# Decode attention plus a gated feed-forward layer on one core: one tile for the gate's activation, and slots for loads that start 32 bytes earlier

## The chip, the core and the metric

The kernel runs on one core of a Trainium2 chip. The core has TensorE (matmuls; PE in the profile, PEld for its loads of weights), VectorE (DVE), ScalarE (ACT), GpSimd (POOL) and SyncE (SP), which here only issues loads. Sixteen DMA engines carry the data between the device's memory and the core's own memory. The core's memory has 128 partitions; a tile has a place in it that is the same byte offset in every partition.

The metric is the device time of one execution in microseconds (us), lower being better.

## The reference, cut to what matters

One token of width 576 is normalised. Attention has 32 heads of width 128 with 16384 cached keys and values each; the feed-forward layer has 4608 hidden units with a tanh-approximated GELU on its gate. All in float32. The output is the sum of the token, the attention and the feed-forward layer.

```python
q = (x @ wq).reshape(B, Sq, H, Dh).transpose(0, 2, 1, 3)          # H, Dh = 32, 128
scores = jnp.einsum("bhqd,bhkd->bhqk", q, k_cache) * (Dh ** -0.5)  # k_cache: 1 x 32 x 16384 x 128
p = _softmax(scores, axis=-1)
o = jnp.einsum("bhqk,bhkd->bhqd", p, v_cache)
A = o.transpose(0, 2, 1, 3).reshape(B, Sq, H * Dh) @ wo

h = _gelu(x @ w_gate) * (x @ w_up)                                  # 576 -> 4608
B = h @ w_down                                                      # 4608 -> 576

xn = _layernorm(x)
return x + A(xn) + B(xn)
```

The K and V caches are 32 x 16384 x 128 x 4 bytes each, 537 MB together, and are read once.

## The kernel before, in words

**Slots.** All large loads go into three slots of 65536 bytes per partition: two of the pool kpool (`kslot()`) and one of the pool vpool (`vslot()`). A load of one head's K or V fills a slot: partition p gets 128 consecutive rows of the cache, 65536 contiguous bytes. The pool cpool lies in front of the slots in each partition and holds the constants and small results; the pool spool (qs, s, the small softmax tiles, o4) lies behind them. A tile takes its bytes rounded up to a multiple of 32. With the tiles of cpool as they are, the first slot starts at byte 27680, the second at 93216 and the third at 158752; each is 32 bytes past a multiple of 1024.

**Loads.** `load()` (L69) issues every large load on SP's queue, in the order of the program. SP waits before a load until its slot is free. Ahead of the heads come the query weights, and the gate and up weights (8 loads; the third slot, `mix`, holds parts of gate and up). Each head has a load of K and one of V (K of head 0 in two halves, so 65 in all). After the heads come the down weights in pieces of 28 and 8 rows and the attention's output weights in pieces of 16, 8, 4, 2, 1 and 1 rows (8 loads), a row being 576 floats of each partition. Inside a slot every one of these loads begins at an offset that is a multiple of 256 bytes.

**One head.** For head h the loop at the end of the main part issues K of h and V of h - 1. Then VectorE multiplies K by the query in place (L215) and sums over the 128 elements of each key (L216); that is `qk`. `softmax` takes the maximum over partitions by way of TensorE (L220 to L226) and lets ScalarE write the exponentials into the tile `pe` (L228, L229), with their sums in a column of `lsum`. `pv` does 32 products of `pe` and V on TensorE (L236) for the head before. V's slot is free when these are done; a slot of K is free when VectorE has summed it. Every four heads `out_heads` collects the result.

**The activation.** `ffn_act` runs once, behind head 0's `qk` on VectorE. Its VectorE steps keep the program's order. It has the gate and up results in `gu` (36 columns of 128 partitions) and makes hT: three steps on VectorE into t1 (L189 to L191), a Tanh on ScalarE from t1 into th (L193), then VectorE's (th + 1) x gate into t2 (L195) and 0.5 x t2 x up into hT (L196).

**The end.** The sums of `lsum` are added over partitions (L300), the heads' results are scaled, and TensorE multiplies by the down and output weights (L281) as their pieces arrive.

Of the kernel before, what the change touches and what calls it, by code (L numbers as in the profile page):

```python
# [8 lines left out]
F32 = mybir.dt.float32  # L9
AF = mybir.ActivationFunctionType  # L10
ALU = mybir.AluOpType
AX = mybir.AxisListType

P = 128
H, SK, DH = 32, 16384, 128
# [11 lines left out]
WD_T = DF // P  # L27
# [7 lines left out]
QUART = D // 4  # L35
HG = 4
PW = 4 * HG
QH = 4


@with_exitstack
def kernel(ctx: ExitStack, tc: tile.TileContext, x, k_cache, v_cache, wq, wo, wg, wu, wd, out):
    nc = tc.nc
    cpool = ctx.enter_context(tc.tile_pool(name="cpool", bufs=1))
# [17 lines left out]
    def kslot():  # L62
        return kpool.tile([P, R * DH], F32, tag="k", name="kslot")

    def vslot():
        return vpool.tile([P, R * DH], F32, tag="v", name="vslot")

    def load(dst, src):
        nc.sync.dma_start(dst, src)  # L69
        return dst  # L70
# [79 lines left out]
    def q_spread(h):  # L150
        r = 32 * (h // (H // 4))
        lo = h % (H // 4) * DH
        pq = ps_s.tile([P, 512], F32, tag="sm", name="pq")
        nc.tensor.matmul(pq, ones[r : r + 1, :], qrow[r : r + 1, lo : lo + QH * DH], start=True, stop=True)  # L154
        return pq

    def q_take(h, pq):
        qs = spool.tile([P, QH, DH], F32, name="qs", bufs=1)
        nc.scalar.activation(qs.rearrange("p h d -> p (h d)"), pq, AF.Copy)
        for i in range(QH):  # L160
            Q[h + i] = qs[:, i : i + 1, :]
# [22 lines left out]
    hT = cpool.tile([P, WD_T], F32, name="hT")  # L184

    def ffn_act():
        g, u = gu[:, 0], gu[:, 1]
        t1 = cpool.tile([P, WD_T], F32, name="t1")
        tc.keep_in_program_order(nc.vector.tensor_mul(t1, g, g))  # L189
        tc.keep_in_program_order(nc.vector.tensor_scalar(t1, t1, 0.044715, 1.0, op0=ALU.mult, op1=ALU.add))  # L190
        tc.keep_in_program_order(nc.vector.tensor_mul(t1, t1, g))  # L191
        th = cpool.tile([P, WD_T], F32, name="th")
        nc.scalar.activation(th, t1, AF.Tanh, scale=0.7978845608028654)  # L193
        t2 = cpool.tile([P, WD_T], F32, name="t2")
        tc.keep_in_program_order(nc.vector.scalar_tensor_tensor(t2, th, 1.0, g, op0=ALU.add, op1=ALU.mult))  # L195
        tc.keep_in_program_order(nc.vector.scalar_tensor_tensor(hT, t2, 0.5, u, op0=ALU.mult, op1=ALU.mult))  # L196

    PO = [ps_o.tile([P, 512], F32, name=f"po{i}") for i in range(2)]
    acc = ps_acc.tile([P, 512], F32, name="acc")
# [3 lines left out]
    S, KT, VT = {}, {}, {}  # L203
    pe = cpool.tile([P, PW - 4 + 32 * PW], F32, name="pe")
    nc.vector.memset(pe, 0.0)
    pe4 = pe[:, PW - 4 :].rearrange("p (k s) -> p k s", s=PW)[:, :, :4]
    lsum = cpool.tile([P, H], F32, name="lsum")
    oall = cpool.tile([P, H], F32, name="oall")

    def qk(h, i, n):  # L210
# [21 lines left out]
    def pv(h):  # L232
        vt, i = VT.pop(h), h % HG
        for k in range(32):
            q, lo = 32 * (k % 4), k * PW + PW - 4 - 4 * i
            nc.tensor.matmul(PO[h // HG % 2][q : q + PW, :], pe[:, lo : lo + PW], vt[:, k * 512 : (k + 1) * 512],  # L236
                             start=i == 0 and k < 4, stop=i == HG - 1 and k >= 28)

    def out_heads(h):
        o4 = spool.tile([P, 512], F32, name="o4", bufs=1)  # L240
        nc.scalar.activation(o4, PO[h // HG % 2], AF.Copy)  # L241
        pc = ps_s.tile([P, 512], F32, tag="sm", name="pc")
        pick = same[:, :PW].rearrange("p (i j) -> p j i", j=4)
        for j in range(4):
# [4 lines left out]
    for h in range(H + 1):  # L249
        if h < H:  # L250
            KT[h], n = kslot(), R if h else SUB
            for i in range(0, R, n):
                load(KT[h][:, i * DH : (i + n) * DH], kv[h][:, i * DH : (i + n) * DH])
        if h > 0:
            VT[h - 1] = load(vslot() if h < H else kslot(), vv[h - 1])
        more = (h + 1) % QH == 0 and h + 1 < H
        pq = q_spread(h + 1) if more else None
        if h < H:
            for i in range(0, R, n):
                qk(h, i, n)  # L260
            KT.pop(h)
        if h == 0:
            ffn_act()
        if h > 0:
            pv(h - 1)
            if h % HG == 0:
                out_heads(h - HG)
        if more:
            q_take(h + 1, pq)
        if h < H:  # L270
            softmax(h)
# [86 lines left out]
```

## Time and profile before

| | us |
|---|---|
| time, median of 3 runs (1369.99 to 1370.04) | 1370.03 |
| the profiled execution's own time | 1370.16 |
| its span, first to last instruction | 1368.3 |
| VectorE busy | 1135.8 (83%) |
| TensorE busy with matmuls | 406.0 (30%) |
| ScalarE busy | 36.5 (3%) |
| moved by DMA | 588.00 MB, 430 GB/s over the span |

The page cuts the span into 40 equal slices; a digit is the busy share of a slice in tenths. A group line names the line of the kernel, the engine, the operation and its tiles; after the first bar come its total busy time and the mean in ns, after the second the idle time of the engine just ahead of it and what ended that. In a line of the chain the first number is the start and the second the duration, both in us. In the timeline, the square bracket gives the idle time before an instruction and what it had waited for. In a line of the windows come the stretch, its length, the busy time of PE, PEld, DVE, ACT and POOL with the number of instructions, the granted clock of TensorE, the share of the DMA engines and their GB/s. In a line of the waits stand the total in us, the number of waits and the longest.

### The profile page before, as it was taken

What the parts mean: (1) busy time and instruction counts of PE and PEld (TensorE: products, weight loads), DVE (VectorE), ACT (ScalarE), POOL (GpSimd) and SP (SyncE); (2) the same over time, 40 slices, a digit from 0 to 9 for tenths busy, and PEclk for the clock granted to TensorE, in tenths of its full rate; (3) what the DMA queues carried; (4) which work ended last, traced back from release to release, by engine and by line L of the source; (5) the groups of instructions that cost most, each with busy time, mean ns of one, the idle gap of its engine ahead of it and who ended that gap; (6) DMA issues with size and microseconds to landing.
All of it is one profiled execution on the core that took longest, in us unless ns stands there. A gap on an engine that the chain in (4) does not pass through costs nothing.

```text
span 1368.3 us, 6377 instructions
## 1 busy us (share of the span) xinstructions
PE 406.0 (30%) x2870; PEld 118.1 (9%) x2870; DVE 1135.8 (83%) x169; ACT 36.5 (3%) x126; POOL 1.0 (0%) x7
## 2 busy tenths in 40 slices
PE   4321233322311232323212332322213333221156
PEld 1110000100000000100000000100001000000012
DVE  1069999899888888898888888998888888988840
ACT  0000000000000000000000000000000000000000
POOL 0000000000000000000000000000000000000000
PEclk8775565565556556565566566565556555665577
DMA  9999999999999999999999999999999999999997
GB/s 404 440 425 450 430 429 430 430 435 432 437 435 429 431 430 439 432 432 435 431 436 433 433 431 430 435 432 439 435 430 430 431 432 437 438 435 428 429 428 336
DMA packets 11704, 588.00 MB, mean 430 GB/s; under 512 B 1303, under 2 KB 1309, under 8 KB 1694
## 3 DMA queue, kind: packets, MB, share of 16 engines
q1 hardware_dynamic: 11664, 587.60, 99.4%
q8 instruction: 22, 0.36, 0.1%
q14 instruction: 4, 0.03, 0.0%
q10 hardware_dynamic: 14, 0.01, 0.0%
HBM read 587.60 MB, written 0.00 MB: 429 GB/s over the span
## 4 chain that ended last, share of the span: by engine, by line
DMA 51%; DVE 46%; PE 2%; issue 0%; SPq 0%; ACT 0%; DVEq 0%
DMA kslot<-in_A_k_cache_dram 41%; DVE s L216 23%; DVE kslot L215 23%; DMA kslot<-in_A_v_cache_dram 3%; DMA kslot<-in_B_w_up_dram 3%; DMA kslot<-in_A_wo_dram 3%; DMA kslot<-in_A_wq_dram 2%; PE pg L139 1%; PE po L236 1%; DVE gu L179 0%; SPq L69 0%; PE pt L222 0%; DVE vslot L176 0%; DVE pm L220 0%; DVE nm L224 0%
## 5 line engine op out<-in xcount | busy, mean ns | idle before, releaser
L215 DVE TENSOR_TENSOR kslot<-kslot,qs 128x16384 f32<-128x16384 f32 (+1 forms) x33 | 551.3, 16705 | 88.4 <-DMA kslot<-in_A_k_cache_dram 86.9
L216 DVE TENSOR_REDUCE s<-kslot 128x128 f32<-128x16384 f32 (+1 forms) x33 | 551.2, 16703 | 3.3
L236 PE MATMUL po<-vslot,pe 128*16 128x512 f32 x1984 | 286.1, 741 | 645.0 <-DMA vslot<-in_A_v_cache_dram 645.0
L236 PEld LDWEIGHTS po<-vslot,pe 128*16 128x16 f32 x1984 | 67.3, 113 | 848.2 <-issue 848.2
L222 PE MATMUL pt<-ident,pm 128*1 128x128 f32 x32 | 11.9, 372 | 236.0 <-DVE pm L220 236.0
L176 DVE TENSOR_TENSOR vslot<-pg,same 128x396 f32<-128x396 f32 (+1 forms) x6 | 3.0, 552 | 69.1 <-PE pg L139 69.1
L139 PE MATMUL pg<-kslot,xnb 128*32 128x396 f32 (+2 forms) x208 | 23.6, 615 | 33.6 <-DMA kslot<-in_B_w_gate_dram 18.9
L228 ACT ACTIVATE nb<-pb 128x1 f32<-128x1 f32 x32 | 5.5, 171 | 812.4 <-PE pb L226 812.4
L320 DVE TENSOR_TENSOR x<-x,po 64x288 f32<-64x288 f32 x1 | 0.5, 457 | 30.8 <-PE po L281 30.8
L222 PEld LDWEIGHTS pt<-ident,pm 128*1 128x1 f32 x32 | 2.5, 79 | 259.4 <-DVE pm L220 218.5
L226 PE MATMUL pb<-nm,ones 1*128 1x1 f32 x64 | 18.1, 350 | 13.2 <-DVE nm L224 13.2
L224 DVE TENSOR_REDUCE nm<-pt 1x1 f32<-1x128 f32 x32 | 8.9, 278 | 14.9 <-PE pt L222 14.9
L226 PEld LDWEIGHTS pb<-nm,ones 1*128 1x128 f32 x64 | 15.8, 305 | 22.2 <-DVE nm L224 11.3
L154 PE MATMUL pq<-qrow,ones 1*128 1x512 f32 x16 | 15.6, 1073 | 0.0
L229 ACT ACTIVATE pe<-s,nb 128x128 f32<-128x128 f32 x32 | 12.8, 401 | 1.0
L302 DVE RECIPROCAL rl<-pl 128x32 f32<-128x32 f32 x1 | 0.4, 358 | 14.9 <-PE pl L300 14.9
L281 PE MATMUL acc<-kslot,oT 128*1 128x144 f32 (+1 forms) x112 | 10.5, 376 | 6.7 <-DMA kslot<-in_A_wo_dram 6.7
L139 PEld LDWEIGHTS pg<-kslot,xnb 128*32 128x32 f32 x208 | 7.1, 126 | 51.0 <-DMA kslot<-in_B_w_gate_dram 19.7
L241 ACT ACTIVATE o<-po 128x512 f32<-128x512 f32 x8 | 4.8, 597 | 222.0 <-PE po L236 222.0
L236 PE MATMUL po<-kslot,pe 128*16 128x512 f32 x64 | 9.6, 769 | 2.6 <-DMA kslot<-in_A_v_cache_dram 2.6
L281 PE MATMUL acc<-vslot,hT 128*1 128x288 f32 x56 | 8.6, 473 | 5.6 <-DMA vslot<-in_B_w_down_dram 5.6
L245 PE MATMUL pc<-same,o 128*128 128x4 f32 x64 | 8.4, 255 | 5.7 <-ACT o L241 5.7
(74 smaller groups left out, 109.9 us busy)
## 6 DMA issues: line engine op xcount, KB each, us to landing
kslot<-in_A_k_cache_dram SPq DMA_DIRECT2D x2, 4096.0 KB
vslot<-in_B_w_down_dram SPq DMA_DIRECT2D x1, 8064.0 KB
kslot<-in_B_w_gate_dram SPq DMA_DIRECT2D x1, 6912.0 KB, 54.0
kslot<-in_B_w_up_dram SPq DMA_DIRECT2D x1, 6912.0 KB
kslot<-in_A_wo_dram SPq DMA_DIRECT2D x1, 4608.0 KB, 39.2
vslot<-in_B_w_gate_dram SPq DMA_DIRECT2D x1, 2304.0 KB, 28.9
vslot<-in_B_w_up_dram SPq DMA_DIRECT2D x1, 2304.0 KB, 37.6
kslot<-in_B_w_down_dram SPq DMA_DIRECT2D x1, 2304.0 KB, 28.7
```

What stands on the lines that cost most here:

```text
L139: nc.tensor.matmul(pg[32 * q : 32 * q + 32, b, :size], lhs, rhs[:, lo : lo + size], start=k == 0, stop=k == len(steps) - 1)
L154: nc.tensor.matmul(pq, ones[r : r + 1, :], qrow[r : r + 1, lo : lo + QH * DH], start=True, stop=True)
L215: tc.keep_in_program_order(nc.vector.tensor_mul(blk, blk, Q[h].to_broadcast([P, n, DH])))
L216: nc.vector.tensor_reduce(S[h][:, i : i + n], blk, axis=AX.X, op=ALU.add)
L222: nc.tensor.transpose(pt[:1, :P], pm, ident)
L224: tc.keep_in_program_order(nc.vector.tensor_reduce(nm, pt[:1, :P], axis=AX.X, op=ALU.max, negate=True))
L226: nc.tensor.matmul(pb[:, :1], ones[:1, :], nm, start=True, stop=True)
L228: nc.scalar.activation(nb, pb[:, :1], AF.Copy, scale=SCALE)
L229: nc.scalar.activation(pe4, S.pop(h).rearrange("p (k s) -> p k s", s=4), AF.Exp, bias=nb, scale=SCALE, accum_out=lsum[:, h : h + 1])
L236: nc.tensor.matmul(PO[h // HG % 2][q : q + PW, :], pe[:, lo : lo + PW], vt[:, k * 512 : (k + 1) * 512], start=i == 0 and k < 4, stop=i == ...
L245: nc.tensor.matmul(pc[:, :HG], o4[:, j * DH : (j + 1) * DH], pick[:, j, :], start=j == 0, stop=j == 3)
L281: nc.tensor.matmul(g, lhs, w[:, i * n : (i + 1) * n], start=id(g) not in seen, stop=last)
```

## The change

Tanh writes back into t1, and the next VectorE step also works in t1, so th and t2 (160 bytes each after rounding) are gone from cpool. `lsum` is made 72 floats (288 bytes) wider, and its first 32 columns are used as before; nothing reads or writes the others. Cpool becomes 32 bytes smaller, and the three slots start at bytes 27648, 93184 and 158720, each a multiple of 1024. The tiles of spool, behind the slots, also move down by 32 bytes. In cpool itself `oall` and t1 move up by 288 bytes, and rl, on and oT down by 32. Each engine has the same instructions in the same order as before.

```diff
+PAD = 72
...
-        th = cpool.tile([P, WD_T], F32, name="th")
-        nc.scalar.activation(th, t1, AF.Tanh, scale=0.7978845608028654)
-        t2 = cpool.tile([P, WD_T], F32, name="t2")
-        tc.keep_in_program_order(nc.vector.scalar_tensor_tensor(t2, th, 1.0, g, op0=ALU.add, op1=ALU.mult))
-        tc.keep_in_program_order(nc.vector.scalar_tensor_tensor(hT, t2, 0.5, u, op0=ALU.mult, op1=ALU.mult))
+        nc.scalar.activation(t1, t1, AF.Tanh, scale=0.7978845608028654)
+        tc.keep_in_program_order(nc.vector.scalar_tensor_tensor(t1, t1, 1.0, g, op0=ALU.add, op1=ALU.mult))
+        tc.keep_in_program_order(nc.vector.scalar_tensor_tensor(hT, t1, 0.5, u, op0=ALU.mult, op1=ALU.mult))
...
-    lsum = cpool.tile([P, H], F32, name="lsum")
+    lsum = cpool.tile([P, H + PAD], F32, name="lsum")[:, :H]
```

## The prediction

> **What bounds the kernel now.** I read the page first, then the chain that ended last in order of time, then the timeline of one head and of the end, and last the waits of the DMA queue. The page:
>
> ```profile
> span 1368.3 us, 6377 instructions
> ...
> PE 406.0 (30%) x2870; PEld 118.1 (9%) x2870; DVE 1135.8 (83%) x169; ACT 36.5 (3%) x126; POOL 1.0 (0%) x7
> ...
> DMA  9999999999999999999999999999999999999997
> GB/s 404 440 425 450 430 429 430 430 435 432 437 435 429 431 430 439 432 432 435 431 436 433 433 431 430 435 432 439 435 430 430 431 432 437 438 435 428 429 428 336
> ...
> q1 hardware_dynamic: 11664, 587.60, 99.4%
> ...
> L215 DVE TENSOR_TENSOR kslot<-kslot,qs 128x16384 f32<-128x16384 f32 (+1 forms) x33 | 551.3, 16705 | 88.4 <-DMA kslot<-in_A_k_cache_dram 86.9
> L216 DVE TENSOR_REDUCE s<-kslot 128x128 f32<-128x16384 f32 (+1 forms) x33 | 551.2, 16703 | 3.3
> ```
>
> The DMA engines are busy in every slice, at 428 to 439 GB/s from the fifth slice to the last but one, and SP's queue q1 alone takes 99.4% of their time. VectorE is the only other engine near it, and it waits for K. The kernel issues 81 large loads on SP (65 of K and V, 8 ahead of them, 8 of down and output weights). 81 x (128 + 16) = 11664, the count in the q1 row: a load is 128 packets, one per partition, and one more for each of the 16 DMA engines. So each engine has 8 rows and one closing packet in a load, 648 rows and 81 closing packets in all.
>
> The windows show that the rate is steady, and the timeline of one head shows that the queue never runs dry:
>
> ```profile
> 200.00:400.00 200.00, 54.58 (x345) 14.97 (x345) 183.11 (x21) 5.29 (x19) 0.00 (x0) 0.59 1.00 431
> ...
> 1000.00:1200.00 200.00, 56.13 (x356) 16.30 (x356) 178.26 (x23) 5.77 (x22) 0.00 (x0) 0.60 1.00 434
> ```
>
> ```profile
> 608.89 0.33 SPq L69 DMA_DIRECT2D vslot<-in_A_v_cache_dram  x1
> 615.48 0.33 SPq L69 DMA_DIRECT2D kslot<-in_A_k_cache_dram  x1
> ...
> 619.62 17.22 DVE L215 TENSOR_TENSOR kslot<-kslot,qs 128x16384 f32<-128x16384 f32 x1 [3.10 <-DMA kslot<-in_A_k_cache_dram]
> 636.95 17.22 DVE L216 TENSOR_REDUCE s<-kslot 128x128 f32<-128x16384 f32 x1
> ...
> 639.10 9.56 PE L236 MATMUL po<-vslot,pe 128*16 128x512 f32 x64 [21.95 <-DMA vslot<-in_A_v_cache_dram]
> ```
>
> A load of V is issued at 608.89, while K is still landing (until 619.6); the next K at 615.48 goes behind that V, which lands at 639.1. So 10.7 and 23.6 us of transfer are ahead of a new issue. What sets the end is therefore the time that the 16 engines need for their packets, and nothing else in the middle of the kernel.
>
> **The price of a row.** The chain gives the times of landing (start plus duration):
>
> ```profile
> 158.46 17.14 DVE kslot L215
> ...
> 193.98 17.14 DVE kslot L215
> ...
> 265.52 42.77 DMA kslot<-in_A_k_cache_dram
> ...
> 342.89 42.84 DMA kslot<-in_A_k_cache_dram
> ...
> 497.77 42.84 DMA kslot<-in_A_k_cache_dram
> ...
> 575.28 44.32 DMA kslot<-in_A_k_cache_dram
> ...
> 1197.89 42.77 DMA kslot<-in_A_k_cache_dram
> ...
> 1275.26 42.84 DMA kslot<-in_A_v_cache_dram
> ...
> 1329.71 35.08 DMA kslot<-in_A_wo_dram
> ```
>
> From 308.29 to 385.73 and from 1240.66 to 1318.10 it is 77.44 us each time, for four loads (two of K, two of V): per engine 2,097,152 bytes, 32 rows of 65536 bytes and 4 closing packets. (Now and then it is 1.5 us more, as 540.61 to 619.60, 78.99; the chain has two such places.) The eight loads at the end have shorter rows, from 64512 down to 2304 bytes: from 1318.10 to the last landing at 1364.79 are 46.69 us, for 1,253,376 bytes per engine, 64 rows and 8 closing packets. Let a byte cost a, and a row with its eighth of a closing packet o:
>
> 77.44 = 2,097,152 a + 32 o; 46.69 = 1,253,376 a + 64 o.
>
> The first times 0.59766 is 46.28 = 1,253,376 a + 19.1 o; the difference is 0.41 = 44.9 o, so o is about 9 ns, and a gives 27.18 GB/s for an engine, 434.9 for 16. A piece of the end agrees:
>
> ```profile
> 1308.00 0.33 SPq L69 DMA_DIRECT2D vslot<-in_B_w_down_dram  x1
> ...
> 1337.21 0.65 PE L281 MATMUL acc<-vslot,hT 128*1 128x288 f32 x2 [5.57 <-DMA vslot<-in_B_w_down_dram]
> ```
>
> 28 rows of 2304 bytes in 128 partitions are 8.258 MB: 18.99 us at 434.9 plus 8 x 9 ns is 19.06, and 1318.10 to 1337.21 is 19.11. So a row costs its bytes and some 9 ns on top, whether it is 2 KB long or 64. These 9 ns, 648 times, are 5.8 us of the span. They are all that a better start of a row can give.
>
> **The change part by part.** The profiled execution took 1370.16 us, its span 1368.3 and 1.86 around it; the median is 1370.03. I subtract from the median.
>
> *The activation in one tile.* The instructions, their engines and their order stay; only operands change: Tanh writes its own input, and the two last VectorE steps read and write the same tile.
>
> ```profile
> L193 ACT ACTIVATE th<-t 128x36 f32<-128x36 f32 x1 | 0.2, 233 | 78.6 <-DVE t L191 78.6
> L191 DVE TENSOR_TENSOR t<-t,gu 128x36 f32<-128x36 f32 x1 | 0.2, 196 | 0.0
> L195 DVE SCALAR_TENSOR_TENSOR t<-th,gu 128x36 f32<-128x36 f32 x1 | 0.2, 196 | 0.3 <-ACT th L193 0.3
> ```
>
> L191 already works in place, and with 196 ns costs what L195 costs with separate tiles. The waits DVE to ACT to DVE are there already, and no other instruction reads the tiles. It runs once, while K of later heads arrives; even 0.2 us more would go into VectorE's slack below. Term: 0, at both ends.
>
> *The padding of lsum.* Nothing reads or writes the 72 columns. Term: 0 by itself. Two tiles of 144 bytes, 160 each when rounded to 32, go, and lsum grows by 288, so the three slots and what lies behind them move down by 32 bytes. Tiles that VectorE reads together with a slot (qs, s) move with it; their distance stays.
>
> *The start of the slots.* All rows of the 81 loads now begin at 32 past a multiple of 256 in the partition (the offsets inside a slot are multiples of 256), and afterwards at such a multiple. No load in this trace lies otherwise, so the price has only bounds. Upper end of the gain: the whole 9 ns of a row is paid for its crooked start and end, 5.8 us. Lower end of a loss: I see none by rows of another position; the nearest price of anything paid per row is again 9 ns, so up to 5.8 us the other way. Between them I take this: a load costs an engine 8 x 9 = 72 ns on top, over 8 rows and a closing packet; if a closing packet costs what a row's top costs, each is 8.0 ns; the closing packets stay, and the rows lose theirs: 648 x 8.0 ns = 5.2 us, hence near 1365. The reason for the high end is the fit itself: the cost is independent of length, as something paid at the two ends of a row would be, and 8 ns is the time of some 220 bytes, what a further short write beside the long one may well take. It is no proof: a price that each packet has by itself looks the same, as every load has rows and closing packets at 8 to 1.
>
> *What is late next.* VectorE: without a wait one head takes it 193.98 - 158.46 = 35.52 us, against 77.44 / 2 = 38.72 us of DMA; 5.2 us less over the kernel is 0.16 us per head, so some 3 us of slack remain. The DMA queue's own waits:
>
> ```profile
> SPq L69 <- DMA vslot<-in_A_v_cache_dram: 695.5, 31, 24.7
> SPq L69 <- PE po L236: 300.3, 32, 10.1
> SPq L69 <- DVE pm L220: 192.5, 31, 13.7
> ```
>
> SP waits for slots to come free, 10 us before the engines would run out; 0.16 us less changes none of it. So the whole term reaches the end: 1370.03 - 5.2 = 1364.8.
>
> **A rule weighed against it.** The Trainium skill, "DMA: Bandwidth & Descriptors", section "How a descriptor splits into AXI transactions", says that a transfer is cut at 256-byte boundaries, that one which starts off such a boundary has one transaction more, and that bytes ahead of the start cost beats of 32 bytes; it tells this of reading. Taken for the writing side, a row of 65536 bytes would have 2049 beats now and 2048 after; by it the gain would be one beat per row, the second case below. No row here shows rows at another position, so the trace bears out neither.
>
> **The rivals.**
> *No change that can be told (within 0.2%, 2.7 us, about what a measurement of this kernel can tell from no change).* The 9 ns is the price of a packet, wherever it begins, and a straight start saves at most the 32 bytes by which it was off: 32 / 27.18 = 1.2 ns, 648 times 0.8 us: 1369.3. For it: closing packets and rows can share the cost evenly. Against it: nothing in the trace. It decides where a row saves less than 2.74 / 648 = 4.2 ns.
>
> *Slower.* With all rows at a multiple of 1024 the 16 engines' writes start alike and get in each other's way at the memory they write; the place is the start of each row, and one more price of 9 ns per row gives 648 x 9 = 5.8 us: 1375.8. It decides from 4.2 ns a row. For it: the 1.5 us jumps show that the engines can be held up. Against it: the rows start alike now as well, 32 bytes further. A slower VectorE would end there too, but L215 and L216 would have to go from 17.22 to over 18.8 us each before the 3.2 us are used up, with distances between their tiles unchanged.
>
> **How the numbers follow.** Faster by the price of the rows, 3 to 5.8 us: 0.47; no change: 0.33; slower: 0.20, because I have no row that excludes it. The prediction is 1364.8, its own range 1363.5 to 1367.3. The full range goes from 1362.8 to 1370.6: below, the whole 5.8 us and another 1.4 us, since 0.1 us in the last landing moves o by 0.1 / 44.9 = 2.2 ns; above, the case without change, with the slower one left out.
>
> **What would show it.** In the chain of the changed kernel, four loads should take 77.44 - 32 x 0.0080 = 77.18 us instead of 77.44, and the end from the last V to the last landing 46.69 - 64 x 0.0080 = 46.18. If both stay within 0.04 us, the second case holds; 77.7 and 47.2 would be the slower one. L215 and L216 should keep 17.22 us, the wait for K shrink from 3.10 to some 2.95 us per head, and L193 and L195 their 0.2 us. The prediction is wrong if a row's 9 ns belong to the packet and not to its position, or if rows that begin at a multiple of 1024 change the rate per byte, which no term here has.

## The result, and the profile after

The changed kernel takes 1366.57 us (median of 10 runs, 1366.40 to 1366.86) against 1370.04 for the kernel before (10 runs, 1369.86 to 1370.28): 3.47 us or 0.25% faster, ratio 0.9975 with a 95% interval of 0.9966 to 0.9983. The forecast was 1364.8 in a range of 1362.8 to 1370.6.

The page of the changed kernel, in the same order as the lines shown of before (VectorE's two lines are L214 and L215 now):

```profile
span 1364.8 us, 6377 instructions
...
PE 405.0 (30%) x2870; PEld 118.1 (9%) x2870; DVE 1135.8 (83%) x169; ACT 36.5 (3%) x126; POOL 1.0 (0%) x7
...
q1 hardware_dynamic: 11664, 587.60, 99.5%
...
L214 DVE TENSOR_TENSOR kslot<-kslot,qs 128x16384 f32<-128x16384 f32 (+1 forms) x33 | 551.3, 16705 | 85.7 <-DMA kslot<-in_A_k_cache_dram 85.7
L215 DVE TENSOR_REDUCE s<-kslot 128x128 f32<-128x16384 f32 (+1 forms) x33 | 551.2, 16703 | 3.3
```

Packets, bytes and VectorE's busy time are as before (1135.8 us, the two large groups to the nanosecond). The span is 3.5 us shorter, and the loads' queue still takes 99.5% of the DMA engines' time. So the same packets took less time. The chain, where each line is start, duration and what was waited for, tells where:

```profile
264.71 42.73 DMA kslot<-in_A_k_cache_dram
...
342.04 42.64 DMA kslot<-in_A_k_cache_dram
...
496.50 42.67 DMA kslot<-in_A_k_cache_dram
...
573.85 43.80 DMA kslot<-in_A_k_cache_dram
...
652.24 42.91 DMA kslot<-in_A_k_cache_dram
...
884.50 42.57 DMA kslot<-in_A_k_cache_dram
...
961.67 42.59 DMA kslot<-in_A_k_cache_dram
...
1271.85 42.88 DMA kslot<-in_A_v_cache_dram
...
1326.44 34.82 DMA kslot<-in_A_wo_dram
```

Start plus duration gives the landings. Four loads take 307.44 to 384.68, that is 77.24 us, or 927.07 to 1004.26, 77.19, where it was 77.44. Some steps are longer, as 617.65 to 695.15 with 77.50, and the jump of before is there too (539.17 to 617.65, 78.48). The gain is spread over the kernel:

| up to the landing of | before | after | gain | rows per engine until then |
|---|---|---|---|---|
| K of head 6 | 308.29 | 307.44 | 0.85 | 168 |
| V of head 31 | 1318.10 | 1314.73 | 3.37 | 584 |
| the last output weights | 1364.79 | 1361.26 | 3.53 | 648 |

That is 5.1, 6.1 and 2.5 ns per row in the three stretches. The last stretch, 46.69 to 46.53 us, is only 64 rows; a tenth of a microsecond more or less there is 1.6 ns per row.

### The profile page after: what moved, and what is told of

It is laid out like the page before. It is cut to its first block, busy times and chain, and to the rows that moved or that the text cites. A ratio compares the mean times of both kernels' runs of the same rounds, so it can differ in the third digit from the quotient of the medians.

```text
span 1364.8 us, 6377 instructions
## 1 busy us (share of the span) xinstructions
PE 405.0 (30%) x2870; PEld 118.1 (9%) x2870; DVE 1135.8 (83%) x169; ACT 36.5 (3%) x126; POOL 1.0 (0%) x7
## 3 DMA queue, kind: packets, MB, share of 16 engines
q1 hardware_dynamic: 11664, 587.60, 99.5%
## 4 chain that ended last, share of the span: by engine, by line
DMA 54%; DVE 43%; PE 2%; issue 0%; SPq 0%; DVEq 0%; ACT 0%
DMA kslot<-in_A_k_cache_dram 44%; DVE s L215 21%; DVE kslot L214 21%; DMA kslot<-in_A_v_cache_dram 3%; DMA kslot<-in_B_w_up_dram 3%; DMA kslot<-in_A_wo_dram 3%; DMA kslot<-in_A_wq_dram 2%; PE pg L140 1%; PE po L235 1%; SPq L70 0%; DVE gu L180 0%; DVE vslot L177 0%; PE pt L221 0%; DVE pm L219 0%; PE acc L280 0%
## 5 line engine op out<-in xcount | busy, mean ns | idle before, releaser
L214 DVE TENSOR_TENSOR kslot<-kslot,qs 128x16384 f32<-128x16384 f32 (+1 forms) x33 | 551.3, 16705 | 85.7 <-DMA kslot<-in_A_k_cache_dram 85.7
L215 DVE TENSOR_REDUCE s<-kslot 128x128 f32<-128x16384 f32 (+1 forms) x33 | 551.2, 16703 | 3.3
L225 PEld LDWEIGHTS pb<-nm,ones 1*128 1x128 f32 x64 | 15.8, 305 | 22.2 <-DVE nm L223 11.3
```

The source lines that it names most:

```text
L214: tc.keep_in_program_order(nc.vector.tensor_mul(blk, blk, Q[h].to_broadcast([P, n, DH])))
L215: nc.vector.tensor_reduce(S[h][:, i : i + n], blk, axis=AX.X, op=ALU.add)
L225: nc.tensor.matmul(pb[:, :1], ones[:1, :], nm, start=True, stop=True)
```

## The experiments

On the chips where these kernels ran, the kernel before took 1370.1 to 1370.2 us. A row is called straight here when it starts at a multiple of 256 bytes, and crooked when it does not; a slot is called the same by its first byte.

**Activation or place.** The activation in one tile stays; the padding is 32 bytes longer, so the slots are back at 27680.

```diff
-PAD = 72
+PAD = 80
```

> The activation in one tile as in the changed kernel, the slots back at byte 27680 (the padding of lsum is 80 columns instead of 72). If the place of the slots is the cause: 1370.0 us as the kernel before, and four loads take 77.44 us again. If the activation were the cause: 1366.6.

Measured: 1370.09 us, ratio 1.0 (0.9991 to 1.0009). Its chain, and the two instructions that changed in the view by line:

```profile
886.68 42.76 DMA kslot<-in_A_k_cache_dram
...
964.04 42.84 DMA kslot<-in_A_k_cache_dram
```

```profile
L193 ACT ACTIVATE t<-t 128x36 f32<-128x36 f32 x1 | 0.2, 233 | 80.5 <-DVE t L192 80.5
...
L194 DVE SCALAR_TENSOR_TENSOR t<-t,gu 128x36 f32<-128x36 f32 x1 | 0.2, 196 | 0.3 <-ACT t L193 0.3
```

From 929.44 to 1006.88 it is 77.44 us again, and Tanh and the step behind it take the same 233 and 196 ns in place as with separate tiles. The activation is worth nothing that these times show (1370.09 us, and 1370.18 for the kernel before on the same chip); the place of the slots is worth all of it. (The small tiles of spool move along with the slots in every kernel here. The runs with more rows, further down, tell the two apart: there the gain grows with the number of rows, while spool moves by the same few bytes.)

**Which multiple.** The same edit with other numbers: 88, 104 and 136 columns, then 64 and 56.

> Slots at byte 27712: 64 past a multiple of 1024. Theory 1, a row pays once for a start off a multiple of 256: 1370.0 us, as with 32. Theory 2, only starts off a multiple of 64 pay: 1366.6. Theory 3, the multiple of 1024 itself matters: 1370.0, which does not part it from theory 1.

> Slots at byte 27776: 128 past a multiple of 1024. Theory 1 (multiples of 256): 1370.0 us. Theory 2 (multiples of 64): 1366.6. A granule of 128 would give 1370.0 at 27712 and 1366.6 here.

> Slots at byte 27904: 256 past a multiple of 1024. Theory 1 (multiples of 256): 1366.6 us. Theory 2 (multiples of 64): 1366.6. Theory 3, a multiple of 512 or 1024 is needed: 1370.0.

> Slots at byte 27616: 224 past a multiple of 256, or 32 ahead of the next, rows unsplit. 32 past gave 1370.1, 64 past 1369.4, 128 past 1369.3. If the odd 32 bytes cost the 0.8 us between these: 1370.1. If the size of the first piece (224 bytes there, 32 here) set it: another time, less or more.

> Slots at byte 27584: 192 past a multiple of 256. By an even multiple of 32 being 0.8 us cheaper than an odd one: 1369.3, as 64 and 128 past.

| first slot at | past a multiple of 256 | time, us | above 1366.57 / 648 rows |
|---|---|---|---|
| 27648 (the changed kernel) | 0 | 1366.57 | 0 |
| 27904 | 0 | 1366.84 | 0.4 ns |
| 27776 | 128 | 1369.28 | 4.2 ns |
| 27712 | 64 | 1369.41 | 4.4 ns |
| 27584 | 192 | 1369.47 | 4.5 ns |
| 27616 | 224 | 1370.03 | 5.3 ns |
| 27680 | 32 | 1370.09 | 5.4 ns |

27904 is no multiple of 512 or 1024 and is as fast to 0.3 us, with short steps in its chain as well (807.23 + 42.70 = 849.93 back to 730.12 + 42.52 = 772.64 are 77.29):

```profile
730.12 42.52 DMA kslot<-in_A_k_cache_dram
...
807.23 42.70 DMA kslot<-in_A_k_cache_dram
```

So 256 is enough, and neither 64 nor 128 is. An odd multiple of 32 costs 0.6 to 0.8 us more than a multiple of 64 that is none of 256, which is about 1 ns per row; of 27712 and 27776 I had expected only 1370.0 or 1366.6. This step is small, but the trace has the duration of every packet, and its rows of 65536 bytes fall into the same groups: 2418.1 ns at 27648 and 27904, 2421.6 to 2421.7 at 27776, 27712 and 27584, 2422.6 at 27616 and 27680 (means of 8192 rows each, without the at most 41 that lie over 20 ns above the median). The size of the first piece does not matter: 32 and 224 past give the same.

**Per row or per byte.** A gain of a quarter per cent could as well be a better rate for every byte. Each load of K and V was split into four, with the slots straight (PAD = 72) and with PAD = 80, which puts them back at 27680.

```diff
+PARTS = 4
...
+    def load_parts(dst, src):
+        w = R * DH // PARTS
+        for i in range(PARTS):
+            load(dst[:, i * w : (i + 1) * w], src[:, i * w : (i + 1) * w])
...
-            for i in range(0, R, n):
-                load(KT[h][:, i * DH : (i + n) * DH], kv[h][:, i * DH : (i + n) * DH])
+            load_parts(KT[h], kv[h])
...
-            VT[h - 1] = load(vslot() if h < H else kslot(), vv[h - 1])
+            VT[h - 1] = vslot() if h < H else kslot()
+            load_parts(VT[h - 1], vv[h - 1])
```

> The changed kernel with each load of K or V split into four, of 16384 bytes per partition: 2176 rows per engine instead of 648, all at multiples of 1024. By the fit of the kernel before, a row costs 9 ns beside its bytes; less the 5.4 ns that a crooked row loses (3.47 us over 648 rows), 3.7 ns are left, and 1528 more rows cost 5.7 us: 1372.3. If a row's own price is still 8 ns, as a fit to the changed kernel's landings gives: 1378.9.

> The same with the slots at byte 27680. Price per row (theory 1): it is 2176 x 5.4 ns = 11.7 us slower than the same split at 27648. Price per byte (a share of the rate): 3.5 us slower, as without the split.

Measured: 1374.97 us at 27648 and 1386.29 at 27680. The first is neither 1372.3 nor 1378.9: 1528 more straight rows cost 8.40 us, 5.5 ns each, between the 3.7 and the 8 that I had worked out. The difference of the two is 11.32 us, 5.2 ns for each of the 2176 rows, where a share of the bytes would have left it at 3.5. The queue's row on the page and two regular steps of the chain, at 27648:

```profile
q1 hardware_dynamic: 39168, 587.61, 100.0%
```

```profile
854.58 38.87 DMA kslot<-in_A_k_cache_dram
...
893.47 38.89 DMA kslot<-in_A_k_cache_dram
```

And at 27680:

```profile
q1 hardware_dynamic: 39168, 587.61, 99.9%
```

```profile
940.53 39.21 DMA kslot<-in_A_k_cache_dram
...
979.76 39.21 DMA kslot<-in_A_k_cache_dram
```

39168 is 272 loads of 144 packets, with the same bytes. A head's K and V take 893.47 - 854.58 = 38.89 us straight and 979.76 - 940.53 = 39.23 crooked: 0.34 us for 64 rows, 5.3 ns each. That the DMA engines stay busy throughout shows that the bound did not move.

The records of single packets agree. At 27680 a row of 16384 bytes takes 615.6 ns in the mean where a straight one takes 611.0. In the kernel before a row of 65536 bytes takes 2422.6 ns and in the changed one 2418.1, a row of 2304 bytes 96.0 and 93.0 (the few rows over 20 ns above the median left out again). So a row 28 times shorter still loses 3 of the 4.5 ns. The closing packets take 9.0 ns in both kernels.

**Halves, as a check of the slope.** Each load of K and V in two equal parts.

> Each load of K or V as two loads of 32768 bytes per partition, slots at 27648: 1152 rows per engine instead of 648, all straight in the slot and in the source. By the quarters (8.4 us for 1528 more rows, 5.5 ns each), 504 more rows cost 2.8 us: 1369.4.

> The same two halves with the slots at byte 27616, all rows crooked in the slot and straight in the source: 1152 x 5.2 ns more than at 27648, so 1375.4.

Measured: 1369.46 and 1375.40 us, both as expected to 0.1 us. Three counts of rows now lie on two lines (the crooked halves have their slots at 27616, the other crooked kernels at 27680):

| rows per engine | straight, us | crooked by an odd 32, us |
|---|---|---|
| 648 | 1366.57 | 1370.09 |
| 1152 | 1369.46 | 1375.40 |
| 2176 | 1374.97 | 1386.29 |
| slope | 5.5 ns | 10.6 ns |
| at no rows | 1363.0 | 1363.2 |

Both lines meet where no rows are: a crooked slot costs nothing but 5.1 ns per row.

**Source against slot, or slot alone.** In all these kernels the source is straight, so a crooked slot also lies differently from its source. Two unequal parts move the cut by 32 bytes, in source and slot alike; with the slots at 27648 and at 27616.

```diff
+CUT = R * DH // 2 + 8
...
+    def load_parts(dst, src):
+        load(dst[:, :CUT], src[:, :CUT])
+        load(dst[:, CUT:], src[:, CUT:])
```

> Slots at 27648, the two parts 32800 and 32736 bytes long: the first ends, the second begins 32 past a multiple of 256, in the source and in the slot alike. If what costs is that source and slot lie differently by 256: 1369.4, as halves at 27648. If each piece of up to 256 bytes that a row touches in the slot costs: one piece more in a pair of rows, 512 x 5.2 ns = 2.7 us: 1372.1. If each row with a crooked end or start costs, 1375.

> Slots at 27616, parts of 32800 and 32736 bytes: in the slot the first part begins 224 past a multiple of 256 and ends at one, the second is straight; in the source the first begins straight and ends 32 past, the second begins 32 past. If source and slot lying differently costs: all rows pay, 1375.4. If the pieces in the slot count: one more in a pair, 1372.1 plus 0.7 us for the 136 other rows, which are crooked: 1372.8.

Measured: 1371.28 and 1371.76 us. At 27616 source and slot lie differently by 224 in every row, yet it is 3.6 us faster than the equal halves there (1375.40); at 27648 they lie alike, yet it is 1.8 us slower than the equal halves (1369.46). So a difference between source and slot is not what costs. Counting the pieces of 256 bytes that a row touches in the slot gives the right order, but too much: one piece more in each of 512 pairs was to cost 2.7 us, and cost 1.8 at 27648, and 2.3 - 0.7 = 1.6 at 27616, some 3.3 ns. (The rows not cut there are 128 and not 136; the 0.7 us stay.) The two times alone cannot part the slot's pieces from the source's, since the cut makes the source crooked too. The packets go a step further. By the straight halves (1213.0 ns for 32768 bytes) and 1.2 ns for 32 bytes, the longer part would take 1214.2 ns and the shorter 1211.8. At 27616 the shorter part begins straight in the slot and 32 past in the source, and takes 1212.2: a crooked start in the source alone adds 0.4 ns. The longer part begins crooked in the slot, ends crooked in the source, and takes 1217.1, which is 2.9 more. What a crooked end costs on either side is not shown, since at 27648 the longer part has it in both and takes 1216.2. Why a piece costs 5.1 ns where one row has a crooked start and end, and 3.3 where a pair shares the cut, stays open.

## Why the prediction was right, point by point

- *What bounds it.* Right. The loads' packets set the end, the queue never ran dry, and all that was saved per packet reached the end. VectorE's durations did not move.
- *The activation and the padding, 0.* Right, by the run with the slots back at 27680.
- *A row has a price beside its bytes, some 9 ns.* Right in kind and slightly low: the slope over the number of rows is 10.6 ns. The miss is within the 2.2 ns that the forecast put on 0.1 us of landing, so that the fit came this near is in part luck. The same fit to the changed kernel's landings (77.24 and 46.53) gives 46.53 - 0.59766 x 77.24 = 0.37, and 0.37 / 44.9 = 8 ns, where the slope is 5.5: two landings of one trace are too coarse for it, and splitting the loads was the better measure.
- *The rows lose all of theirs, 8.0 ns, 5.2 us.* This is the term that was mis-sized: a row loses 5.1 to 5.4 ns, together 3.47 us, and keeps 5.5 ns, with its eighth of a closing packet. I had taken the fixed price of a straight row as nothing but the closing packet's. The closing packets did keep their time, and 9.0 ns each is near the 8.0 assumed. But an eighth of that is at most 1.1 of the 5.5 ns, so a straight row has a price of its own, and the crooked start is half of the whole. That 1364.8 came within 1.8 us of the time is partly two errors against each other: the price was too low and the share of it that goes was too high. With the 10.6 ns of the slope, the same eight ninths would have given 648 x 9.4 ns = 6.1 us, hence 1363.9. And the range reached up to 1370.6, so that a time without any change would have lain in it too; what bears the mechanism out is the runs, not the number.
- *The rivals.* No change within 0.2% would have needed less than 4.2 ns a row; it was 5.4. The 32 bytes alone, 1.2 ns, are about what an odd multiple of 32 costs beside an even one (whether they are its cause was not tried), and not what a start off 256 costs. The slower case found nothing for it: with the rows at a multiple of 1024 the kernel is no slower than at 27904, which is none (1366.57 and 1366.84 us).
- *The rule weighed against it.* The Trainium skill, "DMA: Bandwidth & Descriptors", section "How a descriptor splits into AXI transactions", cuts transfers at 256 bytes. A start off the boundary brings one transaction more for rows like these, whose lengths are multiples of 256 bytes, but not for every transfer: in the section's table one of 96 bytes stays a single transaction. The runs agree with the 256, on the side of the slot. By the count of beats in the Trainium skill a crooked row would have one beat more, which I had put at 0.8 us in all; the measured 3.47 us is over four times that.
- *What would show it.* Four loads were forecast at 77.18 us and took 77.19 to 77.50; the end was forecast at 46.18 and took 46.53, a third of the way from 46.69, and would have decided nothing alone. The wait for K, forecast at 2.95 us per head, varies with the landings:

```profile
617.66 17.22 DVE L214 TENSOR_TENSOR kslot<-kslot,qs 128x16384 f32<-128x16384 f32 x1 [2.99 <-DMA kslot<-in_A_k_cache_dram]
...
695.24 17.23 DVE L214 TENSOR_TENSOR kslot<-kslot,qs 128x16384 f32<-128x16384 f32 x1 [3.30 <-DMA kslot<-in_A_k_cache_dram]
```

## What to carry to other kernels

Where the DMA engines are busy from end to end, count rows as well as bytes: in this kernel a row cost 5.5 ns when it began at a multiple of 256 bytes in the partition and 10.6 ns when it was 32 off, at lengths from 16 to 64 KB, with sources that were straight. One tile of a few bytes ahead of the slots can shift them all, so look at their offset after any edit to the pool in front, and pad to 256 where the loads set the end. Before believing in such a price, multiply what it hangs on, here the number of rows: 3.5 us became 11.3.

## What the runs showed that was not expected

The starts fall into three groups and not two: a multiple of 256 (1366.57 and 1366.84 us), another multiple of 64 (1369.28 to 1369.47), and an odd multiple of 32 (1370.03 and 1370.09). And with the slots straight the landings of four loads no longer repeat: in the kernel before each regular step of the chain is 77.44 us, in the changed one they are 77.19 to 77.27 with some of 77.45 to 77.50 between. Of the 2.52 us gained between K of head 6 and V of head 31, the two jumps bring 0.5 each and the long steps nothing. What holds those steps up, and the jumps of over a microsecond that all these kernels have twice in the chain, was not tried.
